# A fused attention and MLP kernel: score banks, a split exit, and work spread over the slots

## The chip, the cores and the metric

One core of a Trainium2 chip runs the kernel. Times are device microseconds (us) of one execution. The core has five engines, each working through its own queue in order: TensorE (PE; its weight loads are listed as PEld), VectorE (DVE), ScalarE (ACT), GpSimd (POOL) and SyncE (SP), which here only issues DMAs.

## The reference

Inputs are q, k and v of 8 batches x 8 heads x 576 tokens x 64, and an MLP's weights. Each query keeps its 32 highest scores; the softmax over them weighs v; the heads of a token side by side (512 wide) go through 512 -> 2048 -> 512 with a PReLU.

```python
scores = scale * np.matmul(q, k.transpose(0, 1, 3, 2))
kth = np.partition(scores, -32, axis=-1)[..., -32:-31]
scores = np.where(scores >= kth, scores, -1000000000.0)
attn = np.exp(scores - np.max(scores, axis=-1, keepdims=True))
attn = attn / (np.sum(attn, axis=-1, keepdims=True) + 1e-09)
x = np.matmul(attn, v)          # then heads joined: (4608, 512)
h = x @ w_in                    # 512 -> 2048
g = np.maximum(h, 0.0) + alpha * np.minimum(h, 0.0)
out = g @ w_out                 # 2048 -> 512
```

## The kernel before

The work is a list of 144 "duos", one for each turn of the main loop; such a turn is called a slot here. Two heads make a pair, four pairs a batch, and a batch has 18 duos: 16 of kind `("n", p, j)`, the two heads of pair `p` for 128 queries (`j` = 0 to 3), and 2 of kind `("m", p, p+1)`, the last 64 queries of two pairs' four heads. So a duo is always two score blocks of 128 queries x 576 keys. It goes down a pipeline, one stage in each slot; slot `n` does, for different duos:

- PE makes the scores of duo n+2 in fp32 into PSUM tile `ps_sc`, 64 deep (`st_qk`); ACT copies those of n+1 to `s_sb` in SBUF in one instruction (`st_exit`).
- DVE runs 12 MAX8 over the six 96-column pieces of each block of duo n (the results alternate between `up` and `small`, so 6 + 6), and small merges that give a first threshold `p` for each query (`dve_slot`).
- ACT counts by Sign what lies above the threshold of duo n-1 (`sg`, `cs`), POOL multiplies `y = s * sg`, DVE takes the next MAX8 of `y`, picks the exact 32nd value (`pk`) and one slot later sums it to `KT`.
- For duo n-2 ACT makes a Relu mask `r` and POOL subtracts it; for n-3 ACT takes exp to `w` in bf16, and SP issues a DMA transpose to `wT`.
- For duo n-5 PE multiplies `wT` with v and a column of ones (`st_av`, tile `xo`), DVE takes `rz = 1/sum` and normalises to `x`. After four pairs SP transposes `x` to `xT`.

Into these slots the MLP is laid. Tokens that are ready make a chunk (256, 320 or, in the last batch, 128 tokens). An "h unit" is, for one of 16 groups `f` of 128 hidden features, four matmuls into `ph` and DVE's relu of it to `gT` in bf16, in that order in the program (`f_unit`). An "output part" is five matmuls into `pz`, one of x times a combined linear weight `w_lin_b` and four of `gT` times `w_out_b`; after the fourth part of 128 tokens ACT copies `pz` to `o_sb` and SP stores it (`o_unit`). `f_unit` stands at two fixed places of `dve_slot`, `o_unit` before and after `st_qk`; credits of 1.9 and 1.25 a slot (`fo`, `oo`) decide whether one is made. `prep(n, 3)`, the last step of a slot, transposes the k and then the q of a pair of the next batch (4 + 1 PE transposes each, into `tps` and `tpt`, copied out by ACT to `kT` and `qT`) three slots before its first duo. All h units, `tps` and `tpt` share the one buffer of pool `ps_h`. The eight PSUM banks: `ps_sc` 4 (each head's 576 columns start a 1024-column half), `small`, `ps_h`, `ps_z` and `ps_x` 1 each.

Two things set the order. Every instruction goes through the helper `Ordered` (line 31), which keeps each engine's program order, so all rows of the profile bear line L31 and are told apart by their tile names. And within a slot the order is that of the main loop. The weights: four `w_in_b` loads (POOL's queue) before the loop; from slot 1 on, 16 `w_st` loads, each scaled by ACT into `w_out_b` and by POOL into `w_la`; then `w_in_b` is transposed by DMA and 64 matmuls (`plin`) make `w_lin_b`. No h unit or part is made before that is done.

Of the kernel before, what the change touches and what calls it, by code (L numbers as in the profile page):

```python
# [17 lines left out]
NG = 6  # L18
# [17 lines left out]
def fast_path(tc, q, k, v, moe_w_in, moe_w_out, moe_alpha, out, flag):  # L36
# [9 lines left out]
    assert D == 64 and S == 576 and DMODEL == 512 and H == 8 and NFT == 16  # L46
# [7 lines left out]
    for b in range(B):  # L54
        p0 = KPB * b
        duos += [("n", p, j) for j in range(4) for p in range(p0, p0 + KPB)]
        duos += [("m", p0, p0 + 1), ("m", p0 + 2, p0 + 3)]
    ND = len(duos)
    first = {}
    for n, d in enumerate(duos):  # L60
        for p in ((d[1],) if d[0] == "n" else d[1:]):
            first.setdefault(p, n)

    with ExitStack() as ctx:
# [4 lines left out]
        wst = pool("wst", 5)  # L69
        qk_p = pool("qk", 6)  # L70
# [17 lines left out]
        qT, kT, v1 = {}, {}, {}  # L88

        def load_one(p, which, src):  # L90
            t = stg.tile([128, 5, 128], FP32, name=f"{which}_st", tag=f"{which}_st")
            for h in range(2):
                SP.dma_start(t[:, 0:4, 64 * h:64 * h + 64],
                             src[2 * p + h, 0:512, :].rearrange("(c p) d -> p c d", p=128))
            SP.dma_start(t[0:64, 4, :].rearrange("p (h d) -> p h d", h=2),
                         src[2 * p:2 * p + 2, 512:S, :].rearrange("h p d -> p h d"))
            st[which, p] = t

        load_one(0, "k", kv)
        load_one(0, "q", qv)  # L100

# [3 lines left out]
        small = ps_d.tile([128, 512], FP32, name="small")  # L105
        io9 = small[:, 500:509]
        for i in range(9):
            DVE.memset(io9[:, i:i + 1], float(2 * i - 63 + S))
        KT = const.tile([128, ND, 2], FP32, name="KT")
        NV = 8  # L110
        v1s = [const.tile([128, 5, 2, 65], BF16, name=f"v1_{i}") for i in range(NV)]
        ws = [const.tile([128, 2, 640], BF16, name=f"w_{i}") for i in range(3)]
        w_in_b = [const.tile([128, DFF], BF16, name=f"w_in_b{i}") for i in range(4)]
        w_out_b = [const.tile([128, DMODEL], BF16, name=f"w_out_b{i}") for i in range(NFT)]
        w_lin_b = [const.tile([128, DMODEL], BF16, name=f"w_lin_b{i}") for i in range(4)]
        alpha_sb = const.tile([128, NFT], FP32, name="alpha_sb")
        alpha1m = const.tile([128, NFT], FP32, name="alpha1m")
        for t in v1s:
            POOL.memset(t[:, :, :, 64:65], 1.0)
# [3 lines left out]
        def transpose_one(p, which, copy):  # L123
            t = st.pop((which, p))
            dst = qk_p.tile([128, S], FP32, name=f"{which}T", tag=f"{which}T")
            ps = ps_h.tile([128, 512], FP32, name="tps", tag="h")
            for c in range(4):
                PE.transpose(ps[:, 128 * c:128 * c + 128], t[:, c, :], ident_f)
            copy(dst[:, 0:512], ps)
            ps = ps_h.tile([128, 64], FP32, name="tpt", tag="h")  # L130
            PE.transpose(ps, t[0:64, 4, :], ident_f[0:64, 0:64])
            copy(dst[:, 512:S], ps)
            (qT if which == "q" else kT)[p] = dst

        def cast_v(p):
            t = st.pop(("v", p))
            d = v1s[p % NV]
# [6 lines left out]

        def st_qk(n):
            d = duos[n]
            ps = ps_s.tile([128, 2, 1024], FP32, name="ps_sc", tag="s")
            for n0, n1 in ((0, 512), (512, S)):
                if d[0] == "n":
                    _, p, j = d  # L150
                    for i in range(2):
                        r = slice(64 * i, 64 * i + 64)
                        PE.matmul(ps[:, i, n0:n1], qT[p][r, 128 * j:128 * j + 128],
                                  kT[p][r, n0:n1], start=True, stop=True)
                else:
                    for i in range(2):
                        p = d[1 + i]
                        for h in range(2):
                            r = slice(64 * h, 64 * h + 64)
                            PE.matmul(ps[r, i, n0:n1], qT[p][r, 512:S], kT[p][r, n0:n1],  # L160
                                      start=True, stop=True)
            T["ps", n] = ps

        def st_exit(n):
            s = s_p.tile([128, 2, S], FP32, name="s_sb", tag="s")
            ACT.copy(s, T.pop(("ps", n))[:, :, 0:S])
            T["s", n] = s

        def dve_slot(n):
# [3 lines left out]
            on = lambda m: 0 <= m < ND  # L173
            o = 240 * (n % 2)
            if on(n):
                s = T["s", n]
                up = two.tile([128, 2, NG // 2, 8], FP32, name="up", tag="up")
                lo = small[:, o:o + 48].rearrange("p (i g c) -> p i g c", i=2, g=NG // 2)
                top = small[:, o + 48:o + 96].rearrange("p (i g c) -> p i g c", i=2, g=NG // 2)
                hi = small[:, o + 96:o + 112].rearrange("p (i c) -> p i c", i=2)  # L180
                n8 = small[:, o + 112:o + 128].rearrange("p (i c) -> p i c", i=2)
                for i in range(2):
                    for g in range(NG):
                        DVE.max(out=(lo if g % 2 else up)[:, i, g // 2, :],
                                in_=s[:, i, GW * g:GW * g + GW])
                        if i == 0 and g == 1 and on(n - 2):
                            DVE.tensor_reduce(out=KT[:, n - 2, :].unsqueeze(2), in_=T.pop(("pk", n - 2)),
                                              op=ALU.add, axis=AX.X)
# [5 lines left out]
            elif on(n - 2):  # L194
                DVE.tensor_reduce(out=KT[:, n - 2, :].unsqueeze(2), in_=T.pop(("pk", n - 2)),
                                  op=ALU.add, axis=AX.X)
# [10 lines left out]
            if on(n - 1):  # L207
                y, p9, cs = T.pop(("y", n - 1)), T.pop(("p9", n - 1)), T.pop(("cs", n - 1))
                o1 = 240 * ((n - 1) % 2)
                eq = small[:, o1 + 128:o1 + 146].rearrange("p (i c) -> p i c", i=2)  # L210
# [5 lines left out]
            f_unit()  # L216
# [9 lines left out]
            f_unit()  # L226
# [21 lines left out]
        def st_relu(n):  # L248
            s = T["s", n]
            r = two.tile([128, 2, S], BF16, name="r", tag="sg", bufs=3)  # L250
            for i in range(2):
                ACT.activation(r[:, i, :], s[:, i, :], AF.Relu, bias=KT[:, n, i:i + 1], scale=-BIG)
# [14 lines left out]
        def st_av(n):  # L267
            d = duos[n]
            wt = T.pop(("wt", n))
            if d[0] == "n":  # L270
                xo = ps_x.tile([128, 2, 65], FP32, name="xo", tag="x")
                p = d[1]
                for i in range(2):
# [4 lines left out]
            else:  # L278
                xo = ps_x.tile([64, 4, 65], FP32, name="xm", tag="x")
                for i in range(2):  # L280
                    p = d[1 + i]
                    for h in range(2):
                        for c in range(5):
                            K = 128 if c < 4 else 64
                            PE.matmul(xo[:, 2 * i + h, :], wt[0:K, 5 * i + c, 64 * h:64 * h + 64],
# [3 lines left out]
        def block(n):  # L289
            d = duos[n]  # L290
            return (d[1] // KPB, d[2] if d[0] == "n" else 4)
# [3 lines left out]
        def norm_a(n):  # L295
            m, w = (128, 2) if duos[n][0] == "n" else (64, 4)
            rz = two.tile([128, 4], FP32, name="rz", tag="rz")
            DVE.reciprocal(rz[0:m, 0:w], T["xo", n][:, :, 64])
            T["rz", n] = rz

        def norm_b(n):
            d = duos[n]
            xo, rz = T.pop(("xo", n)), T.pop(("rz", n))
            m, w = (128, 2) if d[0] == "n" else (64, 4)
# [518 lines left out]
```

## Time and profile before

| | |
|---|---|
| median of 3 runs | 1343.84 us (1342.06 to 1352.11) |
| the profiled execution's own time | 1352.53 us |
| its span in the trace | 1350.8 us |
| mean granted TensorE clock | 0.808 of 2.4 GHz |
| share of the DMA engines | 35.5% in the hardware queue |

The profiled execution lies 0.6% above the median. The span is what the trace covers; 1.7 us lie around it. TensorE's clock has two levels, 1.0 (2.4 GHz) and 0.5 (1.2 GHz), and the mean says how the time divides.

### The profile page before, as it was taken

What the parts mean: (1) busy time and instruction counts of PE and PEld (TensorE: products, weight loads), DVE (VectorE), ACT (ScalarE), POOL (GpSimd) and SP (SyncE); (2) the same over time, 40 slices, a digit from 0 to 9 for tenths busy, and PEclk for the clock granted to TensorE, in tenths of its full rate; (3) what the DMA queues carried; (4) which work ended last, traced back from release to release, by engine and by line L of the source; (5) the groups of instructions that cost most, each with busy time, mean ns of one, the idle gap of its engine ahead of it and who ended that gap; (6) DMA issues with size and microseconds to landing.
All of it is one profiled execution on the core that took longest, in us unless ns stands there. A gap on an engine that the chain in (4) does not pass through costs nothing.

```text
span 1350.8 us, 18673 instructions
## 1 busy us (share of the span) xinstructions
PE 916.3 (68%) x5228; PEld 484.9 (36%) x5282; DVE 858.1 (64%) x4294; ACT 807.1 (60%) x1337; POOL 771.6 (57%) x677
## 2 busy tenths in 40 slices
PE   3545666777777767777677777677776776667656
PEld 2222233333333333343333333333333333334343
DVE  0866457785568745886468855696568855765631
ACT  1776556675657555775567656585567656645530
POOL 1798447673557545774377635675467645745520
PEclk9999765877778877878678787788688886889867
DMA  7345522253134443345133531534423441423320
GB/s 158 76 112 117 105 51 54 61 114 83 28 65 78 91 85 56 51 98 102 39 71 57 112 78 26 79 70 90 87 50 71 94 97 29 76 46 59 59 52 17
DMA packets 340432, 99.37 MB, mean 74 GB/s; under 512 B 333136, under 2 KB 333152, under 8 KB 340320
## 3 DMA queue, kind: packets, MB, share of 16 engines
q1 hardware_dynamic: 339744, 96.00, 35.5%
q0 software_dynamic: 576, 2.10, 0.8%
q8 instruction: 44, 0.72, 0.2%
q14 instruction: 68, 0.56, 0.1%
HBM read 36.71 MB, written 9.44 MB: 34 GB/s over the span
## 4 chain that ended last, share of the span: by engine, by line
PE 46%; DVE 24%; POOL 9%; ACT 8%; issue 6%; DMA 5%; SPq 1%; ACTq 0%; POOLq 0%
PE pz L31 14%; PE ps_sc L31 13%; PE ph L31 9%; DVE p L31 8%; DVE small L31 6%; POOL y L31 5%; DVE gT L31 4%; PE tps L31 3%; PE xo L31 2%; DVE up L31 2%; ACT sg L31 2%; POOL s_sb L31 2%; DMA wT<-w 2%; PE xm L31 2%; DVE neg L31 2%
## 5 line engine op out<-in xcount | busy, mean ns | idle before, releaser
L31 POOL TENSOR_TENSOR y<-s_sb,sg 128x576 f32<-128x576 f32 x288 | 361.2, 1274 | 435.9 <-ACT sg L31 435.9
L31 POOL TENSOR_TENSOR s_sb<-s_sb,r 128x576 f32<-128x576 f32 x288 | 361.3, 1275 | 97.3 <-ACT r L31 96.7
L31 PE MATMUL ph<-xT,w_in_b 128*128 128x256 bf16 (+3 forms) x1216 | 213.5, 321 | 252.7 <-DVE gT L31 211.9
L31 PE MATMUL ps_sc<-kT,qT 64*128 64x64 f32 (+3 forms) x1280 | 274.6, 563 | 56.4 <-ACT s_sb L31 56.4
L31 ACT ACTIVATE sg<-s_sb,p 128x576 bf16<-128x576 f32 x288 | 220.5, 768 | 95.5 <-DVE p L31 95.3
L31 DVE MAX8 p<-y 128x8 f32<-128x576 f32 x288 | 215.8, 749 | 36.0 <-POOL y L31 36.0
L31 PEld LDWEIGHTS <-w_in_b 128*128 128x128 bf16 x1216 | 114.8, 114 | 308.8 <-issue 254.7
L31 PEld LDWEIGHTS ps_sc<-kT,qT 64*128 64x128 f32 (+1 forms) x1280 | 135.6, 232 | 248.5 <-issue 160.7
L31 ACT ACTIVATE r<-s_sb,KT 128x576 bf16<-128x576 f32 x288 | 207.5, 770 | 24.9 <-DVE KT L31 24.1
L31 DVE MAX8 small<-s_sb 128x8 f32<-128x96 f32 x864 | 216.6, 251 | 0.0
L31 ACT COPY s_sb<-ps_sc 128x1152 f32<-128x1152 f32 x144 | 159.5, 1107 | 89.4 <-PE ps_sc L31 88.9
L31 DVE MAX8 up<-s_sb 128x8 f32<-128x96 f32 x864 | 212.1, 245 | 0.0
L31 PE MATMUL pz<-w_out_b,gT 128*128 128x512 bf16 (+1 forms) x618 | 206.5, 466 | 6.9 <-issue 4.9
L31 DVE RECIPROCAL rz<-xo 128x2 f32<-128x2 f32 x128 | 21.6, 169 | 257.7 <-PE xo L31 257.3
L31 ACT ACTIVATE w<-s_sb 128x1152 bf16<-128x1152 f32 x144 | 165.8, 1151 | 1.2 <-POOL s_sb L31 1.2
L31 DVE TENSOR_SCALAR gT<-ph 128x256 bf16<-128x256 f32 (+2 forms) x244 | 113.6, 466 | 65.8 <-PE ph L31 63.9
L31 PEld LDWEIGHTS <-wT 128*128 128x128 bf16 (+3 forms) x1600 | 99.4, 107 | 80.2 <-DMA wT<-w 34.0
L31 PE MATMUL xo<-v,wT 128*128 128x65 bf16 (+1 forms) x1280 | 108.9, 207 | 6.6 <-DMA wT<-w 5.9
L31 PEld LDWEIGHTS <-gT 128*128 128x128 bf16 (+1 forms) x640 | 76.7, 120 | 88.9 <-issue 48.3
L31 ACT COPY o_sb<-pz 128x512 f32<-128x512 f32 (+1 forms) x40 | 23.2, 581 | 134.3 <-PE pz L31 134.3
L31 ACT COPY kT<-tps 128x512 f32<-128x512 f32 x32 | 18.7, 585 | 127.7 <-PE tps L31 127.7
L31 PE MATMUL pz<-w_lin_b,xT 128*128 128x512 bf16 (+1 forms) x131 | 61.8, 471 | 2.3 <-ACT o_sb L31 2.3
(54 smaller groups left out, 703.9 us busy)
## 6 DMA issues: line engine op xcount, KB each, us to landing
k_st<-in_k_dram SPq DMA_DIRECT2D x64, 128.0 KB, 2.6
q_st<-in_q_dram SPq DMA_DIRECT2D x64, 128.0 KB, 2.6
v_st<-in_v_dram SPq DMA_DIRECT2D x64, 128.0 KB, 2.7
out_dram<-o_sb SPq DMA_DIRECT2D x32, 256.0 KB, 2.2
w_st<-in_moe_w_out_dram SPq DMA_DIRECT2D x16, 256.0 KB, 3.0
wT<-w SPq DMA_TRANSPOSE x144, 3.5
w_in_b<-in_moe_w_in_dram POOLq DMA_DIRECT2D x4, 512.0 KB, 10.2
k_st<-in_k_dram SPq DMA_DIRECT2D x32, 32.0 KB, 2.4
```

The lines of the kernel that those rows point to most:

```text
L31: return self.tc.keep_in_program_order(f(*a, **kw))
```

## The change

- **Scores.** `ps_sc` becomes 1536 columns, three banks: head 0 in columns 0 to 575, head 1 right behind. Five score matmuls in place of four: head 0 to column 512, head 1's first 448 and last 128 columns, and, issued only after ACT has copied head 1, the lone last 64 columns of head 0, which lie in head 1's first bank. The copy out is split: `st_exit_1` (head 1) after the signs, `st_exit_0` (head 0) after the Relu pair; the next scores go into the same tile after that.
- **MLP.** `ps_h` gets two buffers. One h unit a slot, 512 columns wide (two groups `f` of 256 tokens): its matmuls (`h_pe`) stand right after `st_av`, its relu (`h_dve`) later in `dve_slot`. A second unit only while more than 10 wait, and in the end. One output part a slot (`o_pe`), after the lone score matmul, a second while more than 10 wait. Chunks are of 256 tokens; the tails of four batches make one; the last batch runs its tails first and its last two 128-query blocks as chunks of 128.
- **Transposes.** Three pieces a pair (k 4, q 4, both tails 2), at most one piece in a slot, in 12 of a batch's 18 slots, just ahead of the next scores; ACT copies them out after exp, into a joint `qkT`.
- **Loads.** k, q and v of the next batch one array at a time at fixed slots (`at`), and q of pairs 0 and 1 on ACT's queue at the start. `w_in_b` in slots 3, 5, 7 and 9; `w_out` as four 1 MB loads in slots 0, 1, 5 and 9, scaled one group a slot in slots 1 to 16, the second product by DVE in place of POOL; `plin` in slots 17 to 20.

```diff
-        duos += [("n", p, j) for j in range(4) for p in range(p0, p0 + KPB)]
-        duos += [("m", p0, p0 + 1), ("m", p0 + 2, p0 + 3)]
+        full = [("n", p, j) for j in range(4) for p in range(p0, p0 + KPB)]
+        tails = [("m", p0, p0 + 1), ("m", p0 + 2, p0 + 3)]
+        duos += full + tails if b < B - 1 else tails + full
     ND = len(duos)
-    first = {}
-    for n, d in enumerate(duos):
-        for p in ((d[1],) if d[0] == "n" else d[1:]):
-            first.setdefault(p, n)
+    NB = ND // B
...
-        wst = pool("wst", 5)
-        qk_p = pool("qk", 6)
+        qk_p = pool("qk", 2 * KPB)
         s_p = pool("s", 5)
         two = pool("two", 2)
         three = pool("three", 3)
-        gp = pool("gp", 3)
-        xp = pool("xp", 3)
+        gp = pool("gp", 4)
+        xp = pool("xp", 4)
         ps_s = pool("ps_s", 1, space=PSUM)
         ps_d = pool("ps_d", 1, space=PSUM)
-        ps_h = pool("ps_h", 1, space=PSUM)
+        ps_x = pool("ps_x", 1, space=PSUM)
+        ps_h = pool("ps_h", 2, space=PSUM)
         ps_z = pool("ps_z", 1, space=PSUM)
-        ps_x = pool("ps_x", 1, space=PSUM)
...
+        load_one(0, "k", SP)
+        load_one(0, "q", ACT)
+        load_one(1, "k", SP)
+        load_one(1, "q", ACT)
...
+        def prep_pe(p, u):
+            if p not in qkT:
+                qkT[p] = qk_p.tile([128, 2, S], FP32, name="qkT", tag="qkT")
             ps = ps_h.tile([128, 512], FP32, name="tps", tag="h")
-            for c in range(4):
...
+            dst = qkT[p]
+            if u < 2:
+                t = st["kq"[u], p]
+                for c in range(4):
+                    PE.transpose(ps[:, 128 * c:128 * c + 128], t[:, c, :], ident_f)
+                pend.append((dst[:, u, 0:512], ps))
+            else:
+                for i in range(2):
+                    PE.transpose(ps[:, 64 * i:64 * i + 64], st["kq"[i], p][0:64, 4, :], ident_f[0:64, 0:64])
+                pend.append((dst[:, :, 512:S], ps[:, 0:128].rearrange("p (a b) -> p a b", a=2)))
+                del st["k", p], st["q", p]
+        def prep_evac(copy):
+            if pend:
+                d, ps = pend.pop(0)
+                copy(d, ps)
...
+        def qk_part(n, i, n0, n1):
+            d, ps = duos[n], T["ps", n]
+            o = S * i
+            if d[0] == "n":
+                _, p, j = d
+                r = slice(64 * i, 64 * i + 64)
+                return PE.matmul(ps[:, o + n0:o + n1], qkT[p][r, 1, 128 * j:128 * j + 128],
+                                 qkT[p][r, 0, n0:n1], start=True, stop=True)
+            p = d[1 + i]
+            for h in range(2):
+                r = slice(64 * h, 64 * h + 64)
+                PE.matmul(ps[r, o + n0:o + n1], qkT[p][r, 1, 512:S], qkT[p][r, 0, n0:n1],
+                          start=True, stop=True)
...
         def st_qk(n):
-            d = duos[n]
...
+            T["ps", n] = ps_s.tile([128, 1536], FP32, name="ps_sc", tag="s")
+            qk_part(n, 0, 0, 512)
+            qk_part(n, 1, 0, 1024 - S)
+            qk_part(n, 1, 1024 - S, S)
+        def st_exit_1(n):
             s = s_p.tile([128, 2, S], FP32, name="s_sb", tag="s")
-            ACT.copy(s, T.pop(("ps", n))[:, :, 0:S])
+            ACT.copy(s[:, 1, :], T["ps", n][:, S:2 * S])
             T["s", n] = s
-        def dve_slot(n):
-            on = lambda m: 0 <= m < ND
-            o = 240 * (n % 2)
+            qk_part(n, 0, 512, S)
+        def st_exit_0(n):
+            ACT.copy(T["s", n][:, 0, :], T.pop(("ps", n))[:, 0:S])
...
-            f_unit()
+            h_dve()
...
-            f_unit()
+            if f_late:
+                h_pe()
+                h_dve()
...
+        def h_pe():
+            if hq and wi_free and not act:
+                hq.pop(0)()
+        def h_dve():
+            if act:
+                ch, f0, e_n, ph = act.pop(0)
+                DVE.tensor_scalar(ch["g"][:, f0:f0 + e_n, :], ph, 0.0, None, ALU.max)
+                ch["done"] += e_n
+        def o_pe():
+            if lin_done and oq and oq[0][0]["done"] >= oq[0][1]:
+                oq.pop(0)[2]()
...
+        todo = {}
+        def at(slot, kind, f):
+            todo.setdefault((max(0, slot), kind), []).append(f)
+        for b in range(1, B):
+            for i in range(KPB):
+                p = KPB * b + i
+                s0 = NB * (b - 1) + 15 * i // 4
+                at(s0 - 6, "ld", lambda p=p: load_one(p, "k"))
+                at(s0 - 5, "ld", lambda p=p: load_one(p, "q"))
+                at(s0 + 2, "ld", lambda p=p: load_one(p, "v"))
+                at(s0 + 5, "cast", lambda p=p: cast_v(p))
+                for u in range(3):
+                    at(s0 + u, "prep", lambda p=p, u=u: prep_pe(p, u))
+        for p in range(KPB):
+            at(p + 1 + p // 2, "cast", lambda p=p: cast_v(p))
+            if p > 1:
+                at(p, "ld", lambda p=p: load_one(p, "v"))
...
+        at(0, "ld", lambda: out_load(0))
+        at(1, "ld", lambda: out_load(1))
+        at(5, "ld", lambda: out_load(2))
+        at(9, "ld", lambda: out_load(3))
+        for i in range(4):
+            at(3 + 2 * i, "w", lambda i=i: w_in_load(i))
+        for f in range(NFT):
+            at(1 + f, "scale", lambda f=f: scale_out(f))
+        for kk in range(4):
+            at((14, 14, 17, 17)[kk], "ld", lambda kk=kk: in_trans(kk))
+            for a in range(2):
+                at((17, 18, 19, 20)[kk], "lin", lambda kk=kk, a=a: lin(kk, a))
...
+        for n in range(ND + 6):
+            end = n >= ND
+            run(n, "ld")
+            o_sp()
             if on(n - 5):
                 st_av(n - 5)
+            h_pe()
+            run(n, "lin")
+            late = len(hq) > 10 or end
             if on(n - 1):
                 st_count(n - 1)
+                st_y(n - 1)
             if on(n + 1):
-                st_exit(n + 1)
-            if on(n - 1):
-                st_y(n - 1)
-            dve_slot(n)
+                st_exit_1(n + 1)
+            o_pe()
+            run(n, "w")
+            dve_slot(n, late)
             if on(n - 2):
                 st_relu(n - 2)
                 st_sub(n - 2)
+            run(n, "cast")
+            if on(n + 1):
+                st_exit_0(n + 1)
+            if n == 0:
+                prep_all(2)
+            if n == 1:
+                prep_all(3)
+            run(n, "prep", 1)
+            if on(n + 2):
+                st_qk(n + 2)
+            if len(oq) > 10 or end:
+                o_pe()
             if on(n - 3):
                 st_exp(n - 3)
-            casts(n)
-            o_unit()
-            if on(n + 2):
-                st_qk(n + 2)
-            o_unit()
+            while pend:
+                prep_evac(ACT.copy)
+            run(n, "scale")
+            o_act()
             if on(n - 5):
                 st_xT(n - 5)
```

Three places in the order of the instructions. The first is PE at a batch's end, before: the scores of a tail duo, then the transposes of a whole pair, then `xo`.

```order
L31 MATMUL ps_sc<-kT,qT 64x512 x4
L31 MATMUL ps_sc<-kT,qT 64x64 x4
L31 MATMUL tps<-ident_f,k_st 128x128 x4
L31 MATMUL tpt<-ident_f,k_st 128x64
L31 MATMUL tps<-ident_f,q_st 128x128 x4
L31 MATMUL tpt<-ident_f,q_st 128x64
L31 LDWEIGHTS wT
L31 MATMUL xo<-v_3_131,wT 128x65
```

PE now, in a slot with a transpose piece and without an output part:

```order
L31 MATMUL ps_sc<-qkT 128x64
L31 MATMUL tps<-ident_f,q_st 128x128 x4
L31 MATMUL ps_sc<-qkT 128x512
L31 MATMUL ps_sc<-qkT 128x448
L31 MATMUL ps_sc<-qkT 128x128
L31 LDWEIGHTS wT
L31 MATMUL xo<-v_0_133,wT 128x65
```

Between two `xo` there are now 4 transposes at most, and the lone 64-column matmul stands ahead of them; in most slots an output part follows it.

The second is ACT at the same kind of place. Before, four copies of a pair's transposes stand ahead of the signs, and the scores leave in one copy of 1152 columns:

```order
L31 COPY kT<-tps 128x512
L31 COPY kT<-tpt 128x64
L31 COPY qT<-tps 128x512
L31 COPY qT<-tpt 128x64
L31 ACTIVATE sg,cs<-s_sb,p_8582 128x576 x2
L31 COPY s_sb<-ps_sc 128x1152
L31 ACTIVATE r<-s_sb,KT 128x576 x2
L31 ACTIVATE w_137<-s_sb 128x2x576
```

Now:

```order
L31 ACTIVATE sg,cs<-s_sb,p_7945 128x576 x2
L31 COPY s_sb<-ps_sc 128x576
L31 ACTIVATE r<-s_sb,KT 128x576 x2
L31 COPY s_sb<-ps_sc 128x576
L31 ACTIVATE w_142<-s_sb 128x2x576
L31 COPY qkT<-tps 128x2x64
```

The second half of the copy moved behind the Relu pair, and a transpose piece is copied after exp.

The third is DVE between the normalisation and `pk`. Before, two relus of h units:

```order
L31 MAX p_9836<-y 128x8
L31 TENSOR_SCALAR neg<-small 128x2x7
L31 TENSOR_SCALAR gT<-ph 128x256
L31 MAX small<-neg 128x8 x2
L31 MAX p_9836<-y 128x8
L31 TENSOR_SCALAR p_9938<-small 128x2
L31 TENSOR_SCALAR gT<-ph 128x256
L31 SCALAR_TENSOR_TENSOR pk<-small,p_9836 128x18
```

Now, with one:

```order
L31 MAX p_10018<-y 128x8
L31 TENSOR_SCALAR neg<-small 128x2x7
L31 TENSOR_SCALAR gT<-ph 128x512
L31 MAX small<-neg 128x8 x2
L31 MAX p_10018<-y 128x8
L31 TENSOR_SCALAR p_10110<-small 128x2
L31 SCALAR_TENSOR_TENSOR pk<-small,p_10018 128x18
```

One relu of 512 columns stands where there were two of 256 or 320, and its matmuls are no longer issued between DVE's instructions but right behind `xo`.

## Rows read from the trace of the kernel before

**Rows 1.** The page, part 1: busy us (share of the span) and instructions of each engine.

```profile
PE 916.3 (68%) x5228; PEld 484.9 (36%) x5282; DVE 858.1 (64%) x4294; ACT 807.1 (60%) x1337; POOL 771.6 (57%) x677
```

**Rows 2.** Stretches: us, DVE busy on `up` (times; 8 a slot), PE clock, DMA share, GB/s.

```profile
0.00:45.10 45.10, 3.60 (x16) 1.00 0.57 119
45.10:210.90 165.80, 34.21 (x152) 0.86 0.44 94
210.90:1295.20 1084.30, 221.29 (x984) 0.80 0.36 70
1295.20:1350.80 55.60, 0.00 (x0) 0.66 0.18 37
725.50:757.10 31.60, 9.02 (x41) 0.77 0.40 81
```

**Rows 3.** Waits of the whole span: total us, times, longest us.

```profile
DVE rz L31 <- PE xo L31: 257.3, 82, 8.7
PE ph L31 <- DVE gT L31: 211.9, 121, 4.7
```

**Rows 4.** Timeline of a quiet slot: start, us, engine, line, operation [idle before <-releaser].

```profile
746.81 0.17 DVE L31 RECIPROCAL rz<-xo 128x2 f32<-128x2 f32 x1 [0.20 <-PE xo L31]
...
748.48 0.48 DVE L31 TENSOR_SCALAR gT<-ph 128x320 bf16<-128x320 f32 x1
749.01 0.74 PE L31 MATMUL ph<-xT,w_in_b 128*128 128x320 bf16 x4 [1.59 <-DVE gT L31]
...
749.68 2.40 PE L31 MATMUL ps_sc<-kT,qT 64*128 64x512 f32 x8
749.87 0.14 DVE L31 TENSOR_SCALAR p<-small 128x2 f32<-128x2 f32 x1
750.05 0.78 ACT L31 ACTIVATE sg<-s_sb,p 128x576 bf16<-128x576 f32 x1 [0.48 <-DVE p L31]
...
753.11 0.17 DVE L31 RECIPROCAL rz<-xo 128x2 f32<-128x2 f32 x1 [0.25 <-PE xo L31]
```

**Rows 5.** Timeline of a crowded slot, PE's transposes and DVE's next reciprocal.

```profile
654.31 0.66 PE L31 MATMUL tps<-ident_f,k_st 128*128 128x128 f32 x4
...
657.55 0.36 PE L31 MATMUL tpt<-ident_f,q_st 64*128 64x64 f32 x1 [0.68 <-ACT qT L31]
...
658.95 0.17 DVE L31 RECIPROCAL rz<-xo 128x2 f32<-128x2 f32 x1 [6.00 <-PE xo L31]
```

**Rows 6.** Timeline of PE alone in another slot; behind it two windows' clocks (last but two).

```profile
724.65 0.38 PE L31 MATMUL pz<-w_lin_b,xT 128*128 128x512 bf16 x1
...
725.82 1.30 PE L31 MATMUL ps_sc<-kT,qT 64*128 64x512 f32 x8
727.05 0.80 PE L31 MATMUL xo<-v,wT 128*128 128x65 bf16 x10
...
749.70:752.10 2.40, 2.40 (x11) 1.26 (x11) 2.40 (x16) 1.63 (x4) 1.85 (x2) 0.50 0.64 90
725.80:727.10 1.30, 1.30 (x11) 0.74 (x11) 1.30 (x10) 1.17 (x3) 0.00 (x0) 1.00 0.60 110
```

**Rows 7.** Groups by form: busy us, mean ns of one, idle before.

```profile
L31 DVE TENSOR_SCALAR gT<-ph 128x512 bf16<-128x512 f32 x16 | 11.0, 689 | 36.4 <-PE ph L31 36.3
L31 ACT ACTIVATE r<-s_sb,KT 128x576 bf16<-128x576 f32 x288 | 207.5, 770 | 24.9 <-DVE KT L31 24.1 <-DVE rz L31 0.8
L31 ACT COPY s_sb<-ps_sc 128x1152 f32<-128x1152 f32 x144 | 159.5, 1107 | 89.4 <-PE ps_sc L31 88.9
```

**Rows 8.** DMA issues (page, part 6): operation, times, KB each, us to landing.

```profile
wT<-w SPq DMA_TRANSPOSE x144, 3.5
w_in_b<-in_moe_w_in_dram POOLq DMA_DIRECT2D x4, 512.0 KB, 10.2
```

**Rows 9.** Timeline of the start: q's transposes, and DVE's first MAX8.

```profile
18.09 1.08 PE L31 MATMUL tps<-ident_f,q_st 128*128 128x128 f32 x4 [11.70 <-DMA q_st<-in_q_dram]
...
34.07 0.25 DVE L31 MAX8 up<-s_sb 128x8 f32<-128x96 f32 x1
```

More of the change, by code (lines that the diff above doesn't have):

```diff
@@ L326, in st_xT @@
[L326 to L345 removed]
+            d = duos[n]
@@ L347, in unit, with mlp_ready @@
+        hq, oq, act, stores = [], [], [], []
+        def mlp_ready(xt, rows):
+            ntok = sum(r[1] for r in rows)
+            e_n = 512 // ntok
+            ch = {"done": 0}
+            pieces = []
+            for r0, m in rows:
+                for o in range(0, m, 128):
+                    pieces.append((r0 + o, min(128, m - o)))
             def unit(i):
                 if i == 0:
-                    while oq and oq[0][0] <= me - 3:
-                        oq.pop(0)[1]()
-                    hold["g"] = gp.tile([128, NFT, ntok], BF16, name="gT", tag="gT")
@@ L476, in casts @@
-        def casts(n):
-            for p in range(NPAIR):
-                if p not in cast and first[p] <= n - 2:
-                    cast.add(p)
-                    cast_v(p)
-        loads(0, 2)
-        prep(-1, 3)
+                    stores.append((z, t0, pieces))
+            for t0 in range(0, ntok, 128):
+                for a in range(4):
+                    oq.append((ch, 4 * a + 4, lambda t0=t0, a=a: part(t0, a)))
+        def h_pe():
+            if hq and wi_free and not act:
+                hq.pop(0)()
@@ new lines, in h_dve, with o_act @@
+        def h_dve():
[6 more added lines that the diff above has]
+                oq.pop(0)[2]()
+        def o_act():
+            if stores and stores[0][0] is not None:
+                z, t0, pieces = stores.pop(0)
+                o = io.tile([128, DMODEL], FP32, name="o_sb", tag="io")
+                ACT.copy(o, z)
+                at, left = 0, []
+                for r0, m in pieces:
+                    if t0 <= at < t0 + 128:
+                        left.append((r0, at - t0, m))
+                    at += m
+                outs.append((o, left))
@@ new lines, in lin @@
+        def lin(kk, a):
+            if a == 0:
+                hold["z"] = ps_z.tile([128, DMODEL], FP32, name="plin", tag="z")
+            z = hold["z"]
+            for f in range(8 * a, 8 * a + 8):
+                PE.matmul(z, hold["wi", kk // 2][:, f, 128 * (kk % 2):128 * (kk % 2) + 128],
+                          hold["wl", f // 8][:, f % 8, :], start=(f == 0), stop=(f == NFT - 1))
+            if a == 1:
+                ACT.copy(w_lin_b[kk], z)
+                if kk == 1:
+                    wi_free.append(1)
+                if kk == 3:
+                    lin_done.append(1)
@@ new lines, in run, with prep_all @@
+        def run(n, kind, most=99):
+            l = todo.get((n, kind), [])
+            for f in l[:most]:
+                f()
+            if l[most:]:
+                todo.setdefault((n + 1, kind), [])[0:0] = l[most:]
+        for p in (2, 3):
+            load_one(p, "k")
+            load_one(p, "q")
+        for p in (0, 1):
+            load_one(p, "v")
+        SP.dma_start(a16, moe_alpha.rearrange("(t p) -> t p", p=128))
+        copies = [DVE.tensor_copy, ACT.copy]
+        def prep_all(p):
+            prep_pe(p, 0)
+            prep_pe(p, 1)
+            prep_evac(copies[0])
+            prep_evac(copies[1])
+            prep_pe(p, 2)
+            prep_evac(copies[0])
@@ L484, in fast_path @@
+        prep_all(0)
         st_qk(0)
[L485 to L486 removed]
+        st_exit_1(0)
+        st_exit_0(0)
+        prep_all(1)
         st_qk(1)
[L488 to L496 removed]
+        aps = ps_z.tile([128, NFT], FP32, name="aps", tag="z")
```

353 lines of the change are left out of this document (126 added, 227 removed).

## The prediction

> **What bounds the kernel now.** I read four views: the page's first part, the stretches, the waits, and the timeline of single slots. In the page's first part no engine is full: PE is busy 68%, DVE 64%, the others less [rows 1]. So the time is lost in waits, or in an engine that is full only in some slots. The stretches count DVE's operations on `up`, 8 a slot: 19 slots took 165.8 us while the weights were prepared, then 123 slots took 1084.3 us, 8.82 each; but in 725.5 to 757.1 five slots took 31.6, 6.32 each [rows 2]. Slots differ, then, and the mean is far above the good ones. The waits name DVE waiting for PE's `xo`, 257.3 us, and PE waiting for DVE's `gT`, 211.9 us [rows 3]: each engine waits for the other in turn, a loop.
>
> A quiet slot shows that loop [rows 4]. DVE starts the reciprocal at 746.81, does the relu of the first h unit at 748.48; PE can only then use the single `ph` buffer again (749.01, after 1.59 us idle for `gT`), makes the scores (749.68, 2.40 us), then `xo`; the next reciprocal comes at 753.11. That is 6.30 us a round. Whatever PE has besides lies in the same round. In a crowded slot [rows 5] a pair's transposes run from 654.31 to 657.91, 3.60 us, of which four groups of work and copies by ACT alternate on one bank, and DVE stands 6.00 us for `xo`. An output part is 1.17 us on PE (724.65 to 725.82) [rows 6].
>
> **The clock.** The same eight score records took 2.40 us at a granted 0.50 (1.2 GHz) and 1.30 us at 1.00 (2.4 GHz) [rows 6]; over the 123 slots the mean is 0.80 [rows 2].
>
> **Part by part: the steady slots.** The change takes the round apart. Three things can set a slot then, and I work out each.
>
> DVE's own work: the 6.30 us round, less the 0.25 wait at the reciprocal [rows 4], less two relus of 0.48 [rows 4], plus one of 0.69 [rows 7]: 5.78 us.
>
> The new round through ACT and PE. From the threshold `p` the signs start 0.18 us later and take 2 x 0.78 [rows 4]; then half of a copy of 1.11 [rows 7], 0.56 (not shown: it lies between nothing saved, 1.11, and half; I take half, as the copy's columns halve, and add nothing for its start); the lone 64-column matmul, 0.3 (by the 0.36 of the small transpose [rows 5]; up to twice that); an output part 1.17; a transpose piece 0.66 [rows 5]; scores 1.23 and `xo` 0.80 [rows 6]; and from the reciprocal to the next `p` 3.06 less 0.48 plus 0.69 [rows 4, 7], 3.27. `p` of one slot feeds the signs of the next, and `xo` the slot after, so this round spans two slots: 1.74 + 0.56 + 4.16 + 3.27 = 9.73, 4.9 a slot, at 2.4 GHz. At 1.2 GHz scores are 2.40 instead of 1.23, and by the same ratio the part is 2.3; with 0.6, 1.1 and 0.7 to 1.3 for the lone matmul, `xo` and the transposes the round is 12.7 to 13.3, 6.3 to 6.7 a slot. The second copy half stands behind two Relus of 0.77 [rows 7], and the scores wait for it: 0.18 + 1.56 + 0.56 + 1.54 + 0.56 = 4.40 after `p`, where PE's lone matmul, part and transposes end at 2.30 + 0.3 + 1.17 + 0.66 = 4.43. So it is even with them at full clock, and hidden at half.
>
> PE's own work: a unit of 2048 streamed columns, 1.6 times the 0.74 us of 1280 [rows 4], 1.18; `xo` 0.80, the lone matmul 0.3, a part 1.17, two thirds of a 0.66 piece, scores 1.23: 5.1 at 2.4 GHz. At the mean clock of 0.80 that is 6.4. The page bears this out from the other side: PE is busy 916 us [rows 1], the change takes none of that work away, and at the same clock it must fit under the new span.
>
> So DVE wants 5.8, the round 4.9 to 6.7, PE 5.1 to 6.4. I take 6.4: a clock near today's, PE close to full; the five quiet slots show that 6.3 is reached by this kernel already. Bounds: 5.8, if the denser PE gets more of its higher clock, and 6.8.
>
> Two h units with one buffer are gone from the loop, so `gT`'s 211.9 us of PE waits should nearly all go, and the 257.3 of `xo` with them; what is late next is PE itself. POOL loses the weight scaling only; `y` and the subtraction stay (hidden, POOL 57%).
>
> **Exceptions and ends.** 14 tail slots and some 5 slots with a second unit (one more 1.18 and 0.69) cost about 15 us over the whole. Some 17 slots have a second part; they lie inside the 6.4, since other slots have none.
>
> The start: q's first transposes waited 11.70 us for their load and ran at 18.09, and DVE's first MAX8 came at 34.07 [rows 9], because DVE's queue held the q copies of three pairs ahead of it. Now only pairs 0 and 1 are prepared ahead, and q goes on ACT's queue. I put the first MAX8 at 15 to 20 and slot 2 at 31, against 45.1 before [rows 2]; bounds 25 and 45.
>
> Here a shared resource decides. The four 512 KB loads of `w_in_b` took 10.2 us each to land [rows 8], and at the start they stood beside q's load. They move to slots 3, 5, 7 and 9, where the first `wT` transposes run (3.5 us each [rows 8]; `xo` uses one two slots later, so some 8 us of slack). In those stretches I allow nothing, at worst 10.2 once. The Trainium skill, DMA: Bandwidth & Descriptors, section "Issuing engines are not separate DMA queues", says that DMAs issued by ScalarE, SyncE or GpSimd run on the same 16 engines and interleave, so that issuing on several saves only issue time. By that rule q on ACT's queue gains little, and `w_in_b` is felt by `wT` after all: the sum would be up to 10 us higher. The trace's 11.70 us at q leans to the rule.
>
> Slots 2 to 20 had 165.8 us with scaling at two loads a slot and POOL in it. Now a scaling is one ACT and one DVE instruction a slot, some 0.7 each by the rows of 512 to 576 columns [rows 7]. There is no MLP work: 15 slots at 6.0, four with 16 `plin` matmuls each at 8.5, and 7 us for load waits on SP's queue (the loads of slot 0 stand behind waits for the transposes of pairs 1 and 2, and behind them the first `wT`): 131; bounds 115 to 166.
>
> The last stretch, 55.6 us [rows 2], keeps its length: 8 units and 12 parts are left after the last `xo`, about as now; bounds 45 to 65.
>
> Sum of the span: 31 + 131 + 123 x 6.4 + 15 + 56 = 1020. The profiled execution has 1.7 us around its 1350.8 and lies at 1352.53, 0.6% above the median, 1343.84; (1020 + 1.7) x 0.9936 = 1015.
>
> **Rivals.**
> (a) PE is the bound, more than its mean suggests: in-order waits (lone matmul behind ACT, scores behind the second copy, `xo` behind `wT`) add idle time to 6.4 a slot, and the clock stays where it is or falls. For it: PE at 5.1 and DVE at 5.8 are both close to the slot, and a queue in order that serves two masters waits. At 7 to 7.6 a slot: 1089 to 1162. The Trainium skill, TensorE: Matmul & The Clock Gate, section "A second HAM failure mode: psum-queue depth-cycling", tells of a kernel whose cycling through PSUM banks left PE pauses short enough and frequent enough for its clock to swing between the levels. Two `ph` banks and the split scores are such cycling, and by it a mean clock of 0.70 would make PE's 5.1 into 7.3 a slot and the time 1125. The granted clock of 0.77 to 0.80 over many slots [rows 2] lies between its levels, so it swings already.
> (b) DMAs come late: k, q and v loads one at a time, `wT`, `xT` and stores share the engines (36% in the long stretch [rows 2]). If `wT` lands 8 us later than its 3.5 [rows 8] in one slot of eight, that is 1 us a slot: 1138; in one of sixteen 1077. Against it: the traffic is the same as before, only more even.
> (c) The two heads' score passes stop running side by side, since they are now issued as 512, 448, 128 and 64 columns, each alone. Then the 1.23 us of scores becomes up to 2.46, and PE 6.3 at 2.4 GHz, 7.9 at 0.80: about 1199.
> (d) Slower: the clock stays at 1.2 GHz throughout. PE's 5.1 becomes 9.4 by the ratio of the score records (2.40 to 1.30), and 123 x 9.4 gives 1382, over 1343.84. It decides from 9.1 a slot. Against it: the same work now holds 0.80 [rows 2].
> (e) The change does not do what it says: the lone matmul holds PE until ACT has come, slot after slot, and PE waits where DVE waited. Then a slot is the 8.82 of now less the 3.6 us of transposes in 4 of 18 slots, 8.0: 1211.
>
> **How the numbers follow.** The forecast, 940 to 1070, has 0.60: it covers 5.8 to 6.8 a slot with the bounds of the ends. (a) 0.22, (b) 0.06, (c) 0.05, (d) 0.03, (e) 0.04. The predicted time is the forecast's, 1015. The range takes all of the forecast and most of (a) and (b): 940 to 1150, which leaves out some 0.17. A difference of 1% is about what a measurement of this kernel can tell from none; only (d) is on the far side of it: faster 0.95, same 0.02, slower 0.03.
>
> **What the profile after would show.** Right: DVE's wait for `xo` under 100 us, PE's wait for `gT` nearly gone, PE over 80% busy, the gap between first MAX8s of neighbouring slots at 6 to 7 us with few over 9, no transposes over 0.7 us in one piece, the first MAX8 before 20 us. For (a): PE's waits for ACT's `s_sb` copies at over 1 us a slot, or the clock under 0.77. For (b): `xo` waits for `wT`. For (c): score records of `ps_sc` in a slot that sum to 2.4 us at a granted 1.00. Wrong altogether would be a clock that leaves 0.80 by more than 0.1 in either direction, since each term of PE hangs on it, or a chain of waits that runs through POOL, which I have taken as hidden.

## The result and the profile after

The changed kernel takes 994.43 us (median of 4 runs, 993.59 to 995.42), the kernel before on the same chip 1345.71: a ratio of 0.7386, 95% interval 0.7355 to 0.7417. Forecast were 1015 and a range of 940 to 1150.

The page of the changed kernel, part 1, against [rows 1]:

```profile
PE 811.1 (82%) x5202; PEld 477.5 (48%) x5202; DVE 852.3 (86%) x4212; ACT 797.0 (80%) x1443; POOL 748.2 (75%) x661
```

DVE has nearly the same busy time as before and now fills 86% of the span. PE has lost 105 us of busy time with nearly the same number of matmuls, at a mean clock of 0.88 over its span, against 0.81. The stretches, with the columns of [rows 2] (up to slot 2, slots 2 to 20, slots 21 to 143, the rest):

```profile
0.00:33.20 33.20, 3.65 (x17) 1.00 0.75 164
33.20:182.70 149.50, 33.79 (x152) 0.64 0.62 122
182.70:944.80 762.10, 221.03 (x984) 0.92 0.48 95
944.80:993.60 48.80, 0.00 (x0) 0.92 0.32 64
```

The same 123 slots that took 1084.3 us take 762.1, 6.20 each, and PE's clock there is 0.92 in place of 0.80. The same stretch with all engines (busy us of PE, PEld, DVE, ACT, POOL, then clock, DMA share, GB/s), after and before:

```profile
182.70:944.80 762.10, 648.89 (x4340) 382.05 (x4336) 712.52 (x3572) 664.65 (x1206) 633.41 (x541) 0.92 0.48 95
```

```profile
210.90:1295.20 1084.30, 773.66 (x4459) 404.58 (x4506) 731.62 (x3672) 675.50 (x1116) 635.98 (x549) 0.80 0.36 70
```

DVE was busy 67% of it and is now busy 93%: 712.5 / 123 = 5.79 us a slot. The waits of the changed kernel, whole span, with the columns of [rows 3]:

```profile
PE ps_sc L31 <- ACT s_sb L31: 133.2, 147, 2.7
...
DVE rz L31 <- PE xo L31: 35.2, 27, 3.7
ACT w_lin_b L31 <- PE plin L31: 28.2, 4, 8.0
```

DVE's 257.3 us for `xo` became 35.2, and PE's 211.9 for `gT` are gone from the list's top; PE waits for the split exit instead, 133.2 us. In a steady slot without an output part this costs the slot nothing (start, us, engine, operation):

```profile
519.41 0.77 ACT L31 ACTIVATE sg<-s_sb,p 128x576 bf16<-128x576 f32 x1 [0.34 <-DVE p L31]
519.86 1.05 PE L31 MATMUL ph<-xT,w_in_b 128*128 128x256 bf16 x8
...
521.61 0.43 PE L31 MATMUL ps_sc<-qkT 64*128 64x64 f32 x2 [0.70 <-ACT s_sb L31]
521.81 0.16 DVE L31 RECIPROCAL rz<-xo 128x2 f32<-128x2 f32 x1
521.88 0.22 PE L31 MATMUL tps<-ident_f,k_st 64*128 64x64 f32 x1
...
523.48 2.29 PE L31 MATMUL ps_sc<-qkT 64*128 64x512 f32 x6 [1.31 <-ACT s_sb L31]
523.54 0.68 DVE L31 TENSOR_SCALAR gT<-ph 128x512 bf16<-128x512 f32 x1
...
525.30 0.77 ACT L31 ACTIVATE sg<-s_sb,p 128x576 bf16<-128x576 f32 x1 [0.67 <-DVE p L31]
```

From signs to signs 5.89 us. PE idles 0.70 and 1.31 for ACT, yet DVE takes its reciprocal with no wait and goes from one instruction to the next. The median gap between the first MAX8s of neighbouring slots is 5.90. At that length 123 slots would take 726 us; the other 36 lie in some 26 slots of up to 10.3, most of them in waits of DVE for PE (for `xo` 21.2 us in this stretch, for `ph` 7.1).

### The profile page after: what moved, and what is told of

Read it like the earlier page. It is cut to its first block, busy times and chain, and to the rows that moved or that the text cites. A ratio compares the mean times of both kernels' runs of the same rounds, so it can differ in the third digit from the quotient of the medians.

```text
span 993.6 us, 18488 instructions
## 1 busy us (share of the span) xinstructions
PE 811.1 (82%) x5202; PEld 477.5 (48%) x5202; DVE 852.3 (86%) x4212; ACT 797.0 (80%) x1443; POOL 748.2 (75%) x661
## 4 chain that ended last, share of the span: by engine, by line
DVE 61%; PE 20%; ACT 8%; DMA 5%; issue 3%; SPq 1%; POOL 1%; ACTq 0%; DVEq 0%
DVE small L31 21%; DVE p L31 15%; DVE up L31 10%; DVE gT L31 7%; PE pz L31 6%; PE ps_sc L31 6%; PE ph L31 3%; ACT sg L31 3%; DVE neg L31 3%; PE xo L31 3%; ACT r L31 2%; ACT s_sb L31 2%; DMA wT<-w 2%; DVE bot L31 2%; PE plin L31 2%
## 5 line engine op out<-in xcount | busy, mean ns | idle before, releaser
L31 PE MATMUL ps_sc<-qkT 64*128 64x128 f32 (+7 forms) x1280 | 294.4, 506 | 135.6 <-ACT s_sb L31 133.2
L31 PEld LDWEIGHTS ps_sc<-qkT 64*128 64x128 f32 (+1 forms) x1280 | 161.0, 199 | 290.5 <-ACT s_sb L31 192.1
L31 ACT COPY s_sb<-ps_sc 128x576 f32<-128x576 f32 x288 | 179.8, 624 | 37.1 <-PE ps_sc L31 36.8
L31 PE MATMUL ph<-xT,w_in_b 128*128 128x256 bf16 (+1 forms) x1216 | 162.4, 281 | 11.2 <-DMA xT<-x 9.6
L31 PE MATMUL pz<-w_out_b,gT 128*128 128x512 bf16 x576 | 162.4, 407 | 4.6 <-DVE gT L31 4.5
L31 PE MATMUL xo<-v,wT 128*128 128x65 bf16 (+3 forms) x1600 | 136.4, 207 | 15.5 <-DMA wT<-w 15.4
L31 DVE TENSOR_SCALAR gT<-ph 128x512 bf16<-128x512 f32 x144 | 98.1, 681 | 26.2 <-PE ph L31 26.0
L31 PEld LDWEIGHTS <-gT 128*128 128x128 bf16 x576 | 59.1, 103 | 64.1 <-issue 10.6
L31 DVE MAX8 small<-neg 128x8 f32<-128x31 f32 x288 | 56.8, 197 | 5.7
L31 PE MATMUL pz<-w_lin_b,xT 128*128 128x512 bf16 x144 | 59.1, 410 | 0.0
```

The lines of the kernel that those rows point to most:

```text
L31: return self.tc.keep_in_program_order(f(*a, **kw))
```

## Experiments

All are edits of the changed kernel, 4 or 5 runs each (the one profiled among them); unless said otherwise, times are to be held against 994.43.

**The places of PE's work, one part each.** The h unit's matmuls behind the lone score matmul:

```diff
-            h_pe()
             run(n, "lin")
...
                 st_exit_1(n + 1)
+            h_pe()
             o_pe()
```

> Theory A (a steady slot of the changed kernel, 5.9 us, is DVE's own work; PE's order inside it is slack): the h unit's matmuls, moved from right behind xo to behind the lone score matmul, still end before DVE comes to their relu (lone matmul at about 413.3 in the trace, unit 1.1 to 2.0 us, relu place at 415.3): 994 to 1010. Theory B (the early place of the unit's matmuls is what took the loop of DVE and PE apart): DVE waits about 1 us for ph in each slot again, 1060 to 1120.

1009.28 us (ratio 0.7507, with its 95% interval, 0.7466 to 0.7548): 15 us more, theory A's upper end. The early place by itself is worth little.

One bank for units and transposes:

```diff
-        ps_h = pool("ps_h", 2, space=PSUM)
+        ps_h = pool("ps_h", 1, space=PSUM)
```

> One buffer for units and transposes in place of two, nothing else. Theory A: the relu has emptied it 2 to 3 us before the transposes, and the copy out of the transposes ends 1 to 2 us before the next unit, so 994 to 1005. Theory B (the second bank took the loop apart): PE waits for ACT's copy in 12 of 18 slots, about 1 us each, 1060 to 1090.

1026.55 (0.7618, 0.7589 to 0.7646): 32 us, between the two. The usual slot stays at the median of 5.90; single slots grow. Waits of this kernel:

```profile
DVE rz L31 <- PE xo L31: 55.4, 39, 4.3
PE tps L31 <- DVE gT L31: 55.1, 46, 2.4
```

The wait sits where I had excluded it: in the steady slot above PE comes to a transpose piece at 521.88, and the relu that would empty a single bank runs only from 523.54 to 524.22. The transposes come ahead of the relu, not 2 to 3 us after it.

Four score banks, one copy, one bank for the rest:

```diff
+            T["ps", n] = ps_s.tile([128, 2, 1024], FP32, name="ps_sc", tag="s")
+            for n0, n1 in ((0, 512), (512, S)):
+                for i in range(2):
+                    qk_part(n, i, n0, n1)
...
-            ACT.copy(s[:, 1, :], T["ps", n][:, S:2 * S])
+            ACT.copy(s, T.pop(("ps", n))[:, :, 0:S])
             T["s", n] = s
-            qk_part(n, 0, 512, S)
```

> Scores in four banks with one copy of 1152 columns after the signs, and one bank for units and transposes, as before the change; the rest as changed. Theory A: the split exit only moves waits of PE (97.8 us for s_sb in the steady slots), which are not what ends a slot: 985 to 1000, and those waits nearly gone. Theory B (the split exit and the banks carry part of the gain): 1040 to 1120.

1014.65 (0.7535, 0.7506 to 0.7563; runs 1004.7 to 1015.83): 20 us slower than the change, between the two theories, but 12 faster than the split exit with one bank. PE's waits for `s_sb` fell to 55.8 us only, from 87.8 with one bank. So the split exit by itself costs; what it buys is the eighth bank, and that is worth more.

A pair's three pieces in one slot:

```diff
                 for u in range(3):
-                    at(s0 + u, "prep", lambda p=p, u=u: prep_pe(p, u))
+                    at(s0 + 2, "prep", lambda p=p, u=u: (prep_pe(p, u), prep_evac(ACT.copy)))
...
-            run(n, "prep", 1)
+            run(n, "prep")
```

> All three pieces of a pair's transposes in one slot, each copied out at once, 28 such slots. Theory A: in such a slot PE and ACT get about 3 us more, of which the slack of PE takes under 1: about 2.2 us times 28, 1040 to 1070. Rival (scores are made two slots ahead, and that hides it): under 1005.

1032.0 (0.7645, 0.7596 to 0.7694): 38 us, 1.3 for each of 28 slots in place of 2.2: just under theory A's span, whose price was too high, and far above the rival's.

**The MLP's half of a slot.** Two units of 256 columns, still early:

```diff
-            e_n = 512 // ntok
+            e_n = 256 // ntok
...
+            h_dve()
             if f_late:
```

(`h_pe` takes two units, and a slot takes more only when over 20 wait in place of 10, since units are half as large.)

> Two h units of 256 columns a slot in place of one of 512, their matmuls still right behind xo, in the two banks, with two relus in DVE. Theory A (DVE's own work ends a steady slot): two relus of 0.418 us, as 256 columns took before, for one of 0.681 is 0.16 us a slot, some 19 us: 1005 to 1025. Rival (the number of units and relus was itself what cost): over 1080.

1012.45 (0.7521, 0.7469 to 0.7573): 18 us. The number is theory A's, the reason is not. DVE's busy time rises 3.6 us only (855.9) and the median slot stays 5.89; the transposes wait for a relu 52.0 us, nearly as with one bank (55.1), since two units hold both. So the rival is out, and of A only "no loop" is borne out.

The units at their relus, in one bank, as before:

```diff
+            h_pe()
             h_dve()
             if on(n):
...
+            h_pe()
+            h_dve()
             if f_late:
```

(with `e_n = 256 // ntok`, one buffer, no early `h_pe`, and `o_pe` behind `dve_slot`.)

> The MLP half as before the change: two units of 256 columns a slot, each one's matmuls issued only at its relu in DVE's slot, behind the lone score matmul and ahead of the output part, in one bank; scores, exit, transposes and loads as changed. Theory A2 (the gain came from taking this chain, relu, second unit, part, scores, xo, out of the slot): the old quiet round of 6.3 plus a part of 1.2 to 2.2 comes back, 7.5 to 8.2 a slot: 1180 to 1270. Rival (any of it is hidden by slack of PE and only DVE's work counts): 1010 to 1050.

1159.76 (0.8622, 0.8564 to 0.8679): 165 us, the largest effect of one run. 122 steady slots take 896.3 us, 7.35 each, just under theory A2's span and far from the rival's. Its waits in them have the old pair back:

```profile
DVE rz L31 <- PE xo L31: 145.5, 92, 4.4
...
PE ph L31 <- DVE gT L31: 120.6, 130, 1.7
```

The engines' busy times there, with a clock of 0.85:

```profile
188.70:1085.00 896.30, 710.88 (x4256) 411.07 (x4317) 714.97 (x3667) 665.63 (x1200) 628.17 (x537) 0.85 0.40 80
```

DVE's work, 715 us, is about that after the change (707 us in the same 122 slots); the rest is waiting. PE is not full either, 711 of 896 us. The edit holds four parts, and three have a relative above: a later place (15 us), one bank (32), two units (18). They make 65; where the other 100 come from no single part shows. The waits above point to the round of unit, relu, next unit and `xo` itself; the place of the output part, the fourth, was not tried alone.

All three together (the former with the joint exit and pairs at once behind the scores):

> Undoes three parts at once: two units of 256 columns issued at their relus in one bank, scores in four banks with one copy, and a pair's transposes all in one slot behind the scores; loads, chunks, weights and start stay as changed. If the costs only add, 994 + 165 + 20 + 38 = 1217. Theory A2 (all three sit on one round of PE and DVE, where no slack is left once one of them fills it): more than the sum, 1230 to 1320. Rival (they share the same waits): under 1200.

1204.58 (0.8935, 0.8892 to 0.8977): 210 us over the change, just above the rival's span and under theory A2's. The expected sum, 165 + 20 + 38 = 223, counts the loss of the second bank twice, since the run of the units and that of the joint exit both have one bank. Counted once, with the 12 that the joint exit saves on one bank, it is 165 - 12 + 38 = 191, and 210 is more than that; but the pairs' transposes stand elsewhere now, behind the scores. So whether the costs add is not shown. What is left to 1345.71, 141 us, comes from what this kernel keeps: its steady 122 slots take 948.4 us, the same ones before 1079 (from the first MAX8 of slot 21 to that of slot 143, 210.9 to 1289.8), so 130 us lie there, in the chunks' sizes, the parts' places, the loads' or the pairs' slots. No run separates these.

**What ends a steady slot now.** Less work for DVE:

```diff
-                                in_=s[:, i, GW * g:GW * g + GW])
+                                in_=s[:, i, GW * g:GW * g + (GW if g < 4 else 32)])
```

> Leaves out part of the search: the last two of six MAX8 of each block look at 32 columns in place of 96 (so the first threshold is wrong), and the fallback is switched off. Everything but DVE's time is the same. Theory A (DVE's own work ends a steady slot): four instructions shorter by 0.05 to 0.1 each, 0.2 to 0.4 a slot, 965 to 940, until ACT's 5.4 a slot is next. Rival (PE's round, or ACT, ends it already): 985 to 996.

985.12 (0.7317, 0.7268 to 0.7366), with

```profile
PE 796.2 (81%) x5129; PEld 477.5 (49%) x5202; DVE 833.8 (85%) x4212; ACT 796.6 (81%) x1443; POOL 747.0 (76%) x661
```

The time alone lies at the edge of the rival's span and outside theory A's. The short MAX8s took 203 and 175 ns in place of 250 and 246, so DVE's busy time fell by 18.5 us, 0.13 a slot, where I had counted on 0.2 to 0.4. The median slot fell from 5.90 to 5.73: in the usual slot theory A holds. But the time fell by 9.3 us only, half of what DVE saved: DVE's waits for `xo` rose from 35.2 to 41.1, and in the long slots PE is what is late.

Less work for PE:

```diff
-                PE.matmul(z, xt[:, a, t0:t0 + 128], w_lin_b[a], start=(a == 0), stop=False)
```

> Leaves out the linear matmul of every output part (144 of 0.41 us, 59 us of PE), so that the output lacks that term; all else is the same. Theory A (DVE ends a steady slot): only slots where PE is late gain, 980 to 994. Rival (PE is the bound): 935 to 960.

993.56 (0.7368, 0.7316 to 0.742), with

```profile
PE 784.4 (78%) x4988; PEld 469.9 (47%) x5058; DVE 852.9 (85%) x4212; ACT 797.3 (80%) x1443; POOL 747.6 (75%) x661
```

No change (runs 988.99 to 1001.54). PE's busy time fell by 26.7 us, not by the 59 of the matmuls left out, with the clock of the steady stretch at 0.90. Nor do the four executions of the changed kernel follow the clock: means of 0.883, 0.924, 0.881 and 0.902 go with 995.42, 993.59, 994.78 and 994.09 us. So PE's work is not the bound.

**Better versions.** In slots 17 to 20 of the changed kernel DVE stands still; in one of them (timeline):

```profile
144.81 4.82 PE L31 MATMUL plin<-w_la,w_inT 128*128 128x512 bf16 x16
...
149.67 0.59 ACT L31 CAST w_lin_b<-plin 128x512 bf16<-128x512 f32 x1 [7.08 <-PE plin L31]
151.81 0.18 DVE L31 TENSOR_TENSOR small<-small,cs 128x18 f32<-128x18 f32 x1 [5.97 <-ACT sg L31]
```

ACT's queue has the copy of `plin` ahead of the signs. Moved behind exp:

```diff
             if a == 1:
-                ACT.copy(w_lin_b[kk], z)
+                at(17 + kk, "scale", lambda: lin_copy(kk, z))
```

> ACT's copy of w_lin_b out of PSUM in slots 17 to 20 moves from ahead of the signs to behind exp; nothing else. Theory: ACT stands there for plin (28.2 us in four waits) with the signs queued behind, and DVE for the signs (24.7 us), so 15 to 25 us go: 970 to 980. Rival (PE's 16 matmuls in such a slot hold it anyway): 985 to 996.

972.9 (0.7216, 0.7186 to 0.7246): 21.5 us less. Slots 2 to 20 in this kernel, against 149.5 us at a clock of 0.64:

```profile
33.00:159.60 126.60, 91.06 (x450) 51.14 (x446) 110.06 (x544) 109.89 (x201) 103.21 (x94) 0.81 0.74 144
```

The 122 steady slots take 756 us in both.

Then also the loads of v:

```diff
-                at(s0 + 2, "ld", lambda p=p: load_one(p, "v"))
+                at(s0 + (4 if p == KPB else 2), "ld", lambda p=p: load_one(p, "v"))
...
-            at(p + 1 + p // 2, "cast", lambda p=p: cast_v(p))
+            at(p + 1, "cast", lambda p=p: cast_v(p))
```

> The former, and v of the fifth pair loaded two slots later and v of pairs 2 and 3 cast one slot earlier, so that SP no longer stands 13 us for a free v buffer ahead of the first wT. Theory: slots 5 and 7, 9.6 and 8.8 now, fall to 6 to 7: 5 to 8 us less than the former. Rival (wT itself is late behind the weights' loads): under 2 us less.

969.66 (0.7181, 0.7146 to 0.7216): 3 us, less than expected. By the gaps of first MAX8s, slots 5 and 7 fell from 9.6 and 8.7 to 6.3 and 6.2, but slot 3 rose from 6.7 to 9.9. The trace shows where: DVE's scaling of `w_st` into `w_la` took 4.57 us in that slot (at 45.76), against 1.34 in the run before. Six runs above without this edit have such a slot 3 as well (9.3 to 12.4 us; 5.0 for that instruction with one bank and with the joint exit), so it need not be this edit's doing; why it varies stays open.

And the relu by ACT where it has no transposes to copy:

```diff
+            by_act = not late and not todo.get((n, "prep"))
+            dve_slot(n, late, by_act)
...
+            if by_act:
+                h_act()
```

(`h_act` makes the relu by `ACT.activation`, behind exp; DVE's `h_dve` stands only where `by_act` is false.)

> The former, and in slots without a transpose piece (6 of 18) ACT does the unit's relu behind exp in place of DVE. Theory A (DVE's own work ends a steady slot, ACT has 0.4 us left in the mean and more in these slots): 0.68 us less for DVE in some 40 slots, of which half to all shows: 13 to 27 us less than the former. Rival (ACT's round of signs, copies, Relu and exp is as long): 0 to 15 us more.

947.31 (0.7018, 0.6989 to 0.7046), the best: 22 us less, in theory A's span. In the steady stretch DVE and ACT are now level:

```profile
156.80:893.40 736.60, 644.36 (x4323) 379.31 (x4323) 681.09 (x3490) 680.84 (x1250) 625.90 (x536) 0.92 0.48 98
```

## Why the prediction was right, and where it was off

The side and the range held, and so did the account of the kernel before: a round of DVE and PE set the slots, and the change took it apart. Putting the units back into the slot, with one bank, brings back 165 of 351 us and the round's two waits; the bunched transposes bring 38, the joint exit with one bank 20, all three together 210. The other 141 are not traced to a part. What bounds the kernel after was forecast wrongly.

**The steady slots, 802 forecast with their exceptions, 762.1 measured.** The step that was mis-sized is "a clock near today's", and with it "what is late next is PE itself". DVE's 5.8 was right for the usual slot (5.79 busy, 5.90 median gap). PE's 5.1 was divided by 0.80, where the clock was 0.92, which makes 5.5; PE was busy 648.9 us of the 123 slots, 5.28 each, under DVE. (The 5.1 was a little high too: its unit of 1.18 comes from a row at a granted 0.86, and took 1.05 at 1.00, at 519.86.) I took 6.4, the highest of the three, where 5.8, named as the lower bound "if the denser PE gets more of its higher clock", was the case. That PE's work is not the bound is shown by the run that leaves out part of it; that DVE ends the usual slot, by the median of the run with a shorter search.

That 1015 came so near is in part luck. With 5.8 in the sum the steady slots would have been 728 us, 34 too few, since the exceptions, put at 15 us, cost 36 over the median. The 6.4 of a PE that was not the bound covered for them. And by the prediction's own sign, a clock that leaves 0.80 by more than 0.1, its terms of PE were "wrong altogether": 0.92. The usual gap between first MAX8s, 5.90, lies under its 6 to 7 us too; the other signs came (`xo` 35.2 us, `gT` gone, PE at 82%, the first MAX8 at 14.4) but for the one on transposes below.

**Slots 2 to 20, 131 forecast, 149.5 measured.** "Four with 16 `plin` matmuls each at 8.5" counted PE's work and not who queues behind ACT's copy of it: slots 17 to 20 took 10.3, 12.6, 14.4 and 13.8. With the copy moved they took 7.1, 6.6, 7.5 and 7.5, better than my price. The 7 us for load waits were there (slots 5 and 7, 9.6 and 8.8).

**Start and end.** First MAX8 at 14.4 and slot 2 at 33.2, forecast 15 to 20 and 31; the last stretch 48.8 against 56. The errors of the four stretches sum to +2 + 18.5 - 40 - 7, the 26 us by which the span came out below 1020.

**Rivals.** (a) PE does wait for ACT, 97.8 us in the steady slots, 0.80 a slot, under the 1 us that would have spoken for (a). In the slot shown that is slack; but with one bank the split exit cost 12 us over the whole, so it is not free. The steady clock is 0.92 with two `ph` banks and 0.91 with one, so the second `ph` bank did not lower it. The Trainium skill, TensorE: Matmul & The Clock Gate, section "A second HAM failure mode: psum-queue depth-cycling", tells of a kernel that cycled through PSUM banks with pauses of PE, and whose clock swung between its levels. Both runs still go through the score banks, so neither shows the clock without that; the mean of 0.70 did not come. (b) `w_in_b` landed in 6.3 us in the new place, 10.2 before [rows 8], and PE waited 15.4 us for `wT` in all: small. What the Trainium skill, DMA: Bandwidth & Descriptors, section "Issuing engines are not separate DMA queues", says of interleaving isn't judged by this, as q's queue and the place of `w_in_b` changed together. (c) There are four score matmuls for two heads' queries, as before (not five, as the section on the change has it). Three of them still ran side by side: 2.29 us in the slot above, at a granted 0.50, where the four took 2.40 before [rows 4, 6]. The lone fourth comes on top, 0.43 at 521.61: in the 122 steady slots the score records took 235.8 us of PE with the split exit and one bank, 195.9 with the joint exit, at clocks of 0.91 and 0.90. (d) and (e) did not come: a clock of 0.92, and 6.20 a slot.

"No transposes over 0.7 us in one piece" was wrong: a piece of four took 1.06 us at 419.11, at a granted 0.50.

## What to carry to other kernels

Work out each engine's own time and each round of waits for one steady slot; the usual slot takes the largest of them, and the exceptions come on top. A producer that must wait inside the slot for its consumer (unit, relu, unit, scores) costs more than its work. When a change takes such a round apart, don't price the next bound at the old clock alone: here PE ran at 0.92 in place of 0.80, and the other engine became the bound. Then look at what is queued behind each wait in an in-order engine: a copy moved behind other work gave 21.5 us, and moving a relu from the fullest engine in the slots where another has room gave 22.

## What the runs showed of the hardware

The granted clock of PE in the steady slots moved more between kernels than I had allowed: 0.80 before, 0.85 with the units in the slot, 0.90 with the joint exit and 0.92 after, for nearly the same work of PE. Differences of a few hundredths are no more than one kernel shows from run to run (0.88 to 0.92 over the whole span after the change). In slots 2 to 20 it was 0.64 with ACT's copy of `plin` ahead of the signs and 0.81 with it behind exp. What it follows was not tried by itself. Half a copy of scores took 0.624 us, more than half of the whole's 1.107 [rows 7]: splitting it cost ACT 0.14 a slot. MAX8 over 32 columns took 175 to 203 ns, over 96 columns 246 to 250: a third of the columns still takes over two thirds of the time. These records overlap: in a row of MAX8s the next one starts 0.16 us after one of 96 columns and 0.11 to 0.13 after one of 32, and four such savings make the 0.17 of the median slot. One and the same DVE instruction, the third scaling into `w_la`, took 1.34 us in some kernels and up to 5.0 in others; its cause is open.
